# Two-stage attention with a token-mixing MLP: loads moved from two queues with casts in the DMA to one fp32 queue with casts on GpSimd and VectorE

## Chip, cores, metric

One core of a Trainium2 chip. The metric is the device time of one execution in microseconds (us), median of several runs. Each run has a state, fast or slow (slow: over 1.5% above the fastest run of the same kernel on the same chip); comparisons use fast runs. A profile is one execution, and its span is 1.7 to 2.1 us shorter than its run's time.

## The reference

Shapes: batch 8, 8 heads, sequence 576, head dimension 64, 32 latents p per head, model width 512. Everything comes and goes in float32.

```python
def sm_attn(qq, kk, vv):                       # softmax(qq kk^T / 8) vv, per batch and head
    ...
p_packed = sm_attn(p, k, v)                    # 32 latents gather from 576 keys
attn     = sm_attn(q, p_packed, p_packed)      # 576 queries read from 32 latents
x        = attn.transpose(0, 2, 1, 3).reshape(8, 576, 512)
W_tok    = einsum('bsd,btd->bst', x @ w_q, x @ w_k) / 8
out      = maximum(einsum('bst,btd->bsd', W_tok, x), 0) @ w_out
```

## The kernel before

The work of a batch is cut into some forty steps (`kt`: transpose k, `sa`: scores of the latents, `pv`: their weighted sum of v, `qt`/`sc`/`sm`/`at`: the second attention, `wk`/`wq`/`g`/`y`/`mx`: the mixing, `oa`/`ob`: the last product and the store). Each step has a **time** in a table. All steps of all batches are sorted by time plus batch times period, and this sorted list is the program order of every engine. The times order the instructions; they do not delay anything.

```python
    PERIOD = 13.0
    TIMES = {
        "lk": (-17.40,),
        "lq": (-13.25,),
        "vc": (0.00,),
        "kt": (3.88, 5.75, 6.78),
        ...                                                        # cut
    }
    dve_relu = (1, 1, 0, 1)          # 1: VectorE, 0: ScalarE
    dve_out = (0, 0, 1, 1, 0)
    dve_g, dve_y = 1, 1

    def load_k(b):                   # load_q is the same with q
        k_in[b] = inpool.tile([P, NG, R, Dh], bf16, tag="k_sb", name="k_sb")
        nc.gpsimd.dma_start(k_in[b], rows(k, b))      # GpSimd's queue casts fp32 to bf16 in the DMA

    def load_v(b):
        v_in[b] = two.tile([P, NG, R, Dh], fp32, tag="v_in", name="v_in")
        nc.sync.dma_start(v_in[b], rows(v, b))        # SyncE's queue, fp32

    def vc(b, _):
        nc.gpsimd.tensor_copy(v_bufs[b % NV][:, :, :, 0:Dh], v_in[b])
        if b + 2 < B:
            load_v(b + 2)
    ...                                                            # cut
    todo = sorted((t + b * PERIOD, b, name, c)
                  for b in range(B) for name, ts in TIMES.items() for c, t in enumerate(ts))
    with tc.manual_schedule():
        p_transposes(0)              # the p of batches 0 and 1
        n_kt = 0
        for _, b, name, c in todo:
            if b == 0 and name == "pv":
                nc.vector.tensor_copy(p_nat[:, 1:], p_sb[:, 1:])
                for i in range(1, 4):
                    p_transposes(i)  # the p of batches 2 to 7, in front of pv of batch 0
            steps[name](b, c)
            ...                                                    # cut
```

The softmax here doesn't subtract the row's maximum and nothing guards it: scores larger than these inputs give would overflow.

## Time and profile before

| | before |
|---|---|
| time, median (range), 4 runs | 159.64 us (158.26 to 162.23) |
| span of the profile, granted TensorE clock | 159.4 us, 0.959 |
| busy: TensorE, VectorE, ScalarE, GpSimd | 117.9, 103.1, 61.4, 65.3 us |
| DMA, share of 16 engines: casting queue, fp32 queue | 34.3%, 39.7% |
| GpSimd's first weight multiply (L296) of batch 0, of batch 7; end | 29.90, 136.22; 159.4 us |

The times in the last row split the span into a fill, seven periods and a drain. How it, the chain of waits and the windows of this profile are read, the prediction shows.

### The profile page before, as it was taken

Reading aid. Unit: us, or ns where it says so; the run is one execution under the profiler, and the core shown is the slowest. Engines: PE = TensorE matmul, PEld = TensorE weight load, DVE = VectorE, ACT = ScalarE, POOL = GpSimd, SP = SyncE. Lnnn points to the kernel's source line nnn. Section 1 sums busy time; section 2 is a strip of 40 time slices with the busy share of each in tenths; the row PEclk is TensorE's granted clock in tenths of the full one; section 3 lists DMA queues with packets and bytes.
Section 4 is the critical chain, followed back from the end, with each engine's and each line's share of the span. In section 5 each row is a group of like instructions: output and inputs, shape, how many; then the busy total and the mean of one; then the engine's idle time right before and its main releaser. Section 6 shows DMA issues by size and latency. Waiting matters only on the chain.

```text
span 159.4 us, 6466 instructions
## 1 busy us (share of the span) xinstructions
PE 117.9 (74%) x2864; PEld 84.0 (53%) x2864; DVE 103.1 (65%) x239; ACT 61.4 (39%) x130; POOL 65.3 (41%) x72
## 2 busy tenths in 40 slices
PE   1254149828766899489998993799999969978950
PEld 1142137718735686365766862676668657544410
DVE  2538276824594679832997696559859994974630
ACT  3403054701352266024443670257155516433420
POOL 7506700396029703960259229702842350460000
PEclk9999999996999999956999999999999999999996
DMA  4999999999941998399626998995055222536574
GB/s 140 253 349 367 252 312 320 260 213 212 277 175 15 199 248 321 39 236 310 233 70 104 228 333 278 206 219 123 26 128 136 72 66 65 141 86 161 136 208 132
DMA packets 14987, 30.49 MB, mean 191 GB/s; under 512 B 2672, under 2 KB 4464, under 8 KB 14960
## 3 DMA queue, kind: packets, MB, share of 16 engines
q1 hardware_dynamic: 9296, 20.58, 39.7%
q0 software_dynamic: 5664, 9.50, 34.3%
q8 instruction: 22, 0.36, 0.9%
q14 instruction: 5, 0.04, 0.1%
HBM read 30.15 MB, written 9.44 MB: 248 GB/s over the span
## 4 chain that ended last, share of the span: by engine, by line
PE 51%; DVE 17%; issue 12%; DMA 9%; ACT 5%; SPq 2%; DVEq 0%; ACTq 0%
PE out_ps L396 16%; DMA p_sb<-in_p_dram 9%; PE T_ps L200 7%; PE pv_ps L239 7%; PE e_ps L284 4%; DVE relu L354 3%; PE mix_ps L365 3%; PE wq_ps L324 3%; PE aT_ps L305 3%; DVE rs L292 3%; PE e_ps L226 2%; PE wk_ps L313 2%; DVE kT L217 2%; PE g_ps L337 2%; DVE y L108 2%
## 5 line engine op out<-in xcount | busy, mean ns | idle before, releaser
L396 PE MATMUL out_ps<-wout_w,relu 128*128 128x512 bf16 x128 | 36.3, 395 | 0.2 <-issue 0.2
L278 DVE COPY qT<-T_ps 128x768 bf16<-128x768 bf16 x24 | 13.1, 545 | 7.8 <-PE T_ps L200 7.7
L200 PE MATMUL T_ps<-ident,k_sb 128*128 128x128 bf16 x144 | 12.9, 230 | 5.1 <-DVE k_sb L108 3.2
L354 DVE TENSOR_SCALAR relu<-mix_ps 128x512 bf16<-128x512 f32 x24 | 16.0, 667 | 0.4 <-PE mix_ps L365 0.3
L110 ACT ACTIVATE o_sb<-out_ps 128x512 f32<-128x512 f32 x20 | 11.2, 595 | 12.9 <-PE out_ps L396 10.8
L396 PEld LDWEIGHTS <-relu 128*128 128x128 bf16 x128 | 11.5, 102 | 8.6 <-issue 1.6
L217 DVE COPY kT<-T_ps 128x768 bf16<-128x768 bf16 x24 | 12.9, 546 | 4.6 <-PE T_ps L200 4.3
L200 PE MATMUL T_ps<-ident,q_sb 128*128 128x128 bf16 x144 | 13.7, 239 | 0.3 <-DVE qT L278 0.3
L284 PEld LDWEIGHTS <-qT 128*96 128x96 bf16 x192 | 12.1, 124 | 2.9 <-issue 0.2
L200 PEld LDWEIGHTS <-q_sb 128*128 128x128 bf16 x144 | 10.9, 109 | 3.8 <-issue 1.0
L200 PEld LDWEIGHTS <-k_sb 128*128 128x128 bf16 x144 | 9.6, 104 | 6.0 <-DVE k_sb L108 3.7
L108 DVE COPY o_sb<-out_ps 128x512 f32<-128x512 f32 x16 | 10.9, 679 | 2.4 <-ACT o_sb L110 1.8
L356 ACT ACTIVATE rest<-mix_ps 128x256 bf16<-128x256 f32 x8 | 3.1, 384 | 24.0 <-PE mix_ps L372 24.0
L365 PE MATMUL mix_ps<-wqT,y 128*128 128x512 bf16 x32 | 11.8, 385 | 0.4 <-DVE y L108 0.4
L226 PE MATMUL e_ps<-pT,kT 128*32 128x64 bf16 x576 | 9.3, 200 | 2.5 <-issue 1.9
L164 PE MATMUL pT_ps<-ident,p_nat 128*64 128x128 bf16 x32 | 2.3, 313 | 11.2 <-DVE p_nat L429 5.6
L252 POOL TENSOR_TENSOR ppb<-pp,mask 128x256 bf16<-128x256 bf16 x16 | 10.4, 674 | 0.1
L110 ACT ACTIVATE pT<-pT_ps 64x512 bf16<-64x512 bf16 x4 | 4.9, 1255 | 12.0 <-DVE pT L108 12.0
L206 POOL CAST v_bf_85<-v_in 128x2304 bf16<-128x2304 f32 x3 | 6.3, 2113 | 7.3 <-DMA v_in<-in_v_dram 7.3
L307 DVE COPY aT<-aT_ps 128x384 bf16<-128x384 bf16 x24 | 8.3, 346 | 1.3 <-PE aT_ps L305 1.3
L226 PEld LDWEIGHTS <-kT 128*32 128x32 bf16 x576 | 6.2, 100 | 5.5 <-issue 2.2
L313 PE MATMUL wk_ps<-pqk,aT 128*96 128x64 bf16 x96 | 8.7, 217 | 0.2 <-DVE aT L307 0.2
(308 smaller groups left out, 260.2 us busy)
## 6 DMA issues: line engine op xcount, KB each, us to landing
v_in<-in_v_dram SPq DMA_DIRECT2D x8, 1152.0 KB, 10.0
q_sb<-in_q_dram POOLq DMA_DIRECT2D x8, 576.0 KB, 9.2
out_dram<-o_sb SPq DMA_DIRECT2D x24, 192.0 KB, 2.6
k_sb<-in_k_dram POOLq DMA_DIRECT2D x7, 576.0 KB, 7.5
out_dram<-o_sb SPq DMA_DIRECT2D x24, 128.0 KB, 2.6
out_dram<-o_sb SPq DMA_DIRECT2D x24, 64.0 KB, 2.8
k_first<-in_k_dram SPq DMA_DIRECT2D x3, 384.0 KB, 5.8
wout_w<-in_moe_w_out_dram POOLq DMA_DIRECT2D x1, 512.0 KB, 27.6
```

Source lines behind the costliest of these rows:

```text
L108: nc.vector.tensor_copy(o, i)
L110: nc.scalar.activation(o, i, COPY)
L200: nc.tensor.transpose(ps[:, r, G, :], x_sb[:, G, sls[r]:sls[r] + 2, :].rearrange("a r d -> a (r d)"), ident)
L217: nc.vector.tensor_copy(kT, ps)
L226: nc.tensor.matmul(ps[m, r, G], kT[:, r, G, m], pT[:, b, G * NP + pos], start=True, stop=True)
L239: nc.tensor.matmul(ps[m, G, 0:Dh + 1], e1[m, r, G, par, :], v_sb[m, G, s, 0:Dh + 1], start=s == 0 and G == 0, stop=s == R - 1, skip_group_ ...
L278: nc.vector.tensor_copy(qT, ps.rearrange("a r G (pos s) -> a (G pos) r s", s=QP))
L284: nc.tensor.matmul(ps[:, :, h, :], qT[:, h].rearrange("a r s -> a (r s)"), st[b]["ppT"][:, h], start=True, stop=True)
L313: nc.tensor.matmul(ps[:, par, :], st[b]["aT"][:, G, c, par, :], st[b]["pqk"][:, G, Dl:], start=G == 0, stop=G == NG - 1)
L354: nc.vector.tensor_scalar_max(o, i, 0.0)
L365: nc.tensor.matmul(ps, yT[:, j * P:(j + 1) * P], wqT[:, 0:SM], start=True, stop=True)
L396: nc.tensor.matmul(ps, lhsT, wout_w[:, j, :], start=j == 0, stop=j == NJ - 1)
```

## The change

Intent: all loads in fp32 through SyncE's queue, with two staging buffers per tensor, so that GpSimd issues no DMA and k of batch 0 comes first; the casts to bf16 in three pieces per tensor on GpSimd (one piece of q on VectorE); relu, y, g and one output copy per batch to ScalarE; warm-up matmuls in the first batches; new step times that include the casts, among them `pr` for the transposes of the later p groups. The copies behind the transposes of p also get another order of elements (1.2 us each before), and there are fewer output buffers.

```diff
-    PERIOD = 13.0
-    TIMES = { ... }                                   # cut
+    TIMES = (
+        (13.00, {
+            "lk": (-17.28,), "lv": (-11.45,), "lq": (-11.39,),
+            "kc": (-5.13, -4.39, -4.21), "qc": (6.89, 4.50, 3.07), "vc": (0.26, 1.55, -0.98),
+            "kt": (0.00, 0.72, 1.47),
+            ...                                        # cut
+            "pr": (-33.29,),
+        }),
+        (13.04, { "mx": ..., "oa": ..., "ob": ... }),  # cut
+    )
-    dve_relu = (1, 1, 0, 1)
-    dve_out = (0, 0, 1, 1, 0)
-    dve_g, dve_y = 1, 1
+    dve_relu = (0, 0, 0, 0)
+    dve_out = (0, 0, 0, 1, 0)
+    dve_qc = (1, 0, 0)                                 # dve_kc, dve_vc, dve_a2: all 0
+    dve_g, dve_y = 0, 0
+    def load(x, name, b, pieces=1):
+        x_in[name, b] = t = two.tile([P, NG, R, Dh], fp32, tag=name + "_in", name=name + "_in")
+        n = R // pieces
+        for c in range(pieces):
+            nc.sync.dma_start(t[:, :, c * n:(c + 1) * n], rows(x, b)[:, :, c * n:(c + 1) * n])
+    def cast(dve, o, i):
+        (nc.vector if dve else nc.gpsimd).tensor_copy(o, i)
     nc.sync.dma_start(p_sb[:, 0], p_v[:, 0])
+    for x, name in ((k, "k"), (v, "v"), (q, "q")):
+        load(x, name, 0, NC3)
+    ...                                                # the weights; cut
     nc.sync.dma_start(p_sb[:, 1:], p_v[:, 1:])         # the rest of p: last of the first loads
     def p_transposes(g):
+        nc.vector.tensor_copy(p_nat[:, g], p_sb[:, g])
+    def pr(b, _):
+        if b % 2 == 1 and b + 1 < B:
+            p_transposes((b + 1) // 2)
     with tc.manual_schedule():
+        constants()
+        warm_up(4)
         p_transposes(0)
+        warm_up(5)
         for _, b, name, c in todo:
-            if b == 0 and name == "pv": ...            # the p groups 1 to 3; cut
             steps[name](b, c)
+            if (b, name) in early:                     # most steps of batch 0, kt and sa of batch 1
+                warm_up(1)
```

## The prediction

> **What bounds the kernel now.** I read the page first (chain of work that ended last, groups, DMA queues), then the chain in order of time, then the waits, the table of windows and the timelines of GpSimd and TensorE. The page's chain, by engine, says that no one thing is the bound: half of it is TensorE, but 12% is "issue" (TensorE waits for nothing that the profile shows) and 9% is one DMA.
>
> ```profile
> PE 51%; DVE 17%; issue 12%; DMA 9%; ACT 5%; SPq 2%; DVEq 0%; ACTq 0%
> ```
>
> The chain in order of time (start, length, what) shows where these lie.
>
> ```profile
> 3.72 15.13 DMA p_sb<-in_p_dram
> 18.87 0.57 DVE p_nat L429
> ...
> 23.34 2.10 PE pv_ps L239 x125
> ...
> 32.72 3.60 issue
> ...
> 97.14 2.94 issue
> ```
>
> **Fill.** The rest of p is the last of the first loads. It lands at 18.87 us, and three groups of p's transposes stand in TensorE's order before the first pv step, so pv of batch 0 ends at 25.4 us although its scores were ready at 13.6 us. The first attention weight (GpSimd's tensor_tensor of L296) starts at 29.90 us, that of the last batch at 136.22 us, and the span ends at 159.4 us. So the kernel is a fill of 29.9 us, seven periods of 15.2 us (106.3 / 7) and a drain of 23.2 us.
>
> **Period.** What is the least that TensorE needs per batch? From the chain and the groups at full clock: 36 transposes at 0.34 us per six (2.04), e of L226 3 x 0.36 (1.08), pv 1.2, e of L284 3 x 0.34 (1.02), aT 0.5, wk 0.5, wq 0.5, g 0.35, y 0.22, mix 1.1, ppT and pqk 0.33, and 18 out matmuls at 0.215 us (3.87). Together 12.7 us. The windows (columns: length, busy of PE, PEld, DVE, ACT, POOL with counts, granted clock, DMA share, GB/s) show how near the good stretches are, and what spoils the others.
>
> ```profile
> 96.00:98.00 2.00, 1.14 (x79) 0.68 (x77) 1.90 (x6) 0.00 (x0) 2.00 (x3) 1.00 1.05 397
> 98.00:100.00 2.00, 0.00 (x0) 0.00 (x0) 0.40 (x1) 0.00 (x0) 1.98 (x4) 1.00 0.64 102
> 38.00:40.00 2.00, 2.00 (x21) 1.87 (x20) 1.28 (x5) 0.57 (x2) 0.51 (x1) 0.50 1.13 215
> 117.00:131.00 14.00, 12.70 (x353) 9.34 (x352) 11.36 (x28) 6.49 (x15) 4.81 (x6) 1.00 0.38 97
> ```
>
> The last line is a batch with few loads left: 14 us, PE busy 12.7, VectorE 11.4. The first two are a stall: pv stops between two matmuls of one group whose inputs have long been ready, for 2.94 us, right where DMA is full. The third is the other loss: after the 3.60 us stall at 32.72 the granted clock is 0.50, and again at 68 to 74 us.
>
> **Between stages VectorE is a second bound**: from 76.5 to 85 us the chain runs almost wholly through it (kT, rs, relu, o_sb). The costliest of its groups that the change touches:
>
> ```profile
> L354 DVE TENSOR_SCALAR relu<-mix_ps 128x512 bf16<-128x512 f32 x24 | 16.0, 667 | 0.4 <-PE mix_ps L365 0.3
> L206 POOL CAST v_bf_86<-v_in 128x2304 bf16<-128x2304 f32 x3 | 6.3, 2114 | 0.0
> q1 hardware_dynamic: 9296, 20.58, 39.7%
> q0 software_dynamic: 5664, 9.50, 34.3%
> q8 instruction: 22, 0.36, 0.9%
> ```
>
> The queues are at 75% of 16 engines' span together, some 119 us. q8 is the third witness for the stalls: 22 packets of 16 KB are about TensorE's 5,728 instructions at 64 bytes.
>
> **What the Trainium skill says.** (1) "Runtime: NRT & Kernel Launch", section "Instruction fetch mechanics": instructions are streamed in 16 KiB blocks of 256 by DMA and the cost is mostly hidden. The trace agrees on the blocks (0.36 MB in 22 packets) and not on the hiding, if I read the stalls rightly: 0.3 to 0.7 us at pv where DMA is light (114.4, 128.1), 2.9 and 3.6 us where it is full. (2) "SBUF — State Buffer", the box on the SWDGE trap and the shared port pair: a DMA issued from GpSimd needs GpSimd to write descriptors, and a VectorE op in a two-port mode (an fp32 SBUF to SBUF copy) and a GpSimd op shut each other out for a whole instruction. In the trace each GpSimd DMA takes 0.75 us of that engine; nothing in it is long enough to show the lock, since VectorE casts from SBUF only at the start. (3) "DMA: Bandwidth & Descriptors", section "Issuing engines are not separate DMA queues": moving transfers to another queue gives no bandwidth. The trace agrees: full-share windows move 206 to 221 GB/s of bf16 in the casting queue (twice that in fp32 read) and 397 to 410 GB/s in fp32 loads. (4) "TensorE: Matmul & The Clock Gate", Part 1: the clock is halved after an idle window of about 3.4 us. The trace agrees at 38 us, and at 98 us a stall of 2.94 us did not trip it.
>
> **The change part by part.**
> - Fill. The rest of p goes behind k, v, q and the weights, and its transposes behind pv of batch 0. Loads in order: p 0.13 MB lands at 2.9 us as before, then k 1.18 MB at 400 GB/s without the casting queue beside it: about 6 us (the third piece landed at 10.1 before), v 9 us, q 12 us. GpSimd casts k in three pieces (a third of 2.11, 0.70 us each) behind its memsets: about 7 to 9 us. kT and scores by 10, v cast by 11.5, pv until 13 (warm, 1.2 instead of 2.1), q cast 12 to 13.5, sc at 15, exp 0.6, sums and reciprocal 0.9: first weights at about **17.5 us** instead of 29.9, so 12.4 us gained. The warm-up matmuls run in TensorE's idle time.
> - VectorE per batch: less three relu (16.0 us in all), y (5.1), g (2.4), one of two o_sb per batch (5.4), memsets about 2; plus one cast of q at 0.57 (4.6 in all). 103.1 - 30.9 + 4.6 = 76.8, or 9.6 us per batch.
> - ScalarE gets them: 61.4 + 24 x 0.595 + 8 x 0.595 + 4.8 + 2.1 = 87.4, or 10.9 per batch.
> - GpSimd: 65.3 less 13.5 of DMA issues and 16.8 of casts, plus 64 casts of about 0.73 (46.7), 2 for w_out, 3 of memsets: 86.7, or 10.8 per batch. It is near the others but below TensorE.
> - DMA: 28.3 MB of loads at 400 GB/s are 71 us, p and weights 4, stores 9.44 MB at 215 / 0.79 = 272 GB/s are 35: 110 us, or 13.2 per batch in steady state (8.85 + 4.3). Nearly the period itself.
> - Period. TensorE is now the longest engine but DMA: 12.7 plus bubbles, some 13.6 us (14.1 in the good batches before, when VectorE had 11.4). In the first two periods the 5 us of mix and out of earlier batches are missing, but loads (9 us) and GpSimd (10.8) are not: about 12. The lag of a batch's output behind its attention grows by some 7 us in the step times, which fits this.
> - Stalls of instruction fetch: 0.3 to 3.6 before, DMA now busy nearly always, but one data queue instead of two. I choose 1.3 us per period, 9 in all.
> - Drain: at the last weights there is work left of about out of 5, mix and out of 6 and 7 and the tail of attention 7: 3 x 3.87 + 2 x 1.1 + 3.5 = 17.3 us, against about 15.5 before with a drain of 23.2. So 24 to 25.
>
> **Sum**: 17.5 + 2 x 12 + 5 x 13.6 + 9 + 24 = 142.5 of span, and the median lay 0.9 over the profiled span: **143 us**, 17 less than 160.25. Of the 17, 12 come from the fill and some 5 to 6 from the periods (15.2 to 14.4).
>
> **The rivals.**
> - *Instruction fetch takes over.* For it: DMA at 13.2 us per batch is full through the middle, and the worst stalls were in full stretches, one of them (97 us) beside fp32 loads of the SyncE queue, just what will be the rule. Against: stalls lie in pv and the dense scores, and the new times set 12 long matmuls between these. At 3 us per period instead of 1.3, with a clock drop or two: about 155.
> - *GpSimd becomes the bound.* Its casts and weights are in one order; a cast that waits for a late load holds the weights behind it, and VectorE's q cast and GpSimd exclude each other (0.6 us per batch). For it: 10.8 of 13, loads of v and q bunched, stores in the same queue behind them. Against: loads are issued 10 to 14 us ahead. At 15 us per period: 17.5 + 105 + 24 = 146 to 148.
> - *All goes as the step times would have it.* TensorE full, no clock loss, 11.5 in the first two periods and 13 after, fetch hidden: 17.5 + 23 + 65 + 4 + 23 = 133.
> - *Nothing gained*: the early start only shifts the wait to the loads. Against: loads end at 110 us of DMA time whatever the order, well under 143.
>
> **Range and chances.** The second rival and the third mark the sides, the first is the worse tail: 134 to 152. Within 2% or slower would need the fill's 12 us to be lost again in stalls: 0.04 and 0.02. Faster 0.94.
>
> **What would show it.** First weights on GpSimd at 16 to 20 us (fill right); their spacing about 12 in the first two periods and 14 to 15 in the later; PE busy over 12.5 per period; DVE near 77, ACT 87, POOL 87 busy; no software_dynamic queue and DMA share near 1 from 3 to about 85 us; "issue" at pv, near 1.3 us per batch and longer where DMA is full. The prediction is wrong if GpSimd's casts are much over 0.73 us, if GpSimd waits for loads in the middle, or if TensorE waits on kT, qT or v for more than 1 us per batch.

## More of the kernel before

The granted clock is a mean over the clock events that the trace records. The stretch before the first event (26.8 us in before) is counted as full clock, although TensorE's transposes took some 314 ns in it, against 219 later; so the mean is too high.

## The result, and the profile after

| | before | after |
|---|---|---|
| time, median (range), 4 runs each | 159.64 us (158.26 to 162.23) | 171.03 us (169.68 to 173.66) |

The ratio is **1.072** (95% interval 1.057 to 1.087): slower by 7%, where 143 us had been predicted. Ratios here and below are the mean time of one kernel's fast runs over that of the other's fast runs of the same rounds, so not quite the ratio of the medians.

The first profile of the changed kernel fell in the slow state (span 171.9 us, clock 0.887). The kernel was run again unaltered (a_again), and its profile is what is read here. It is the quickest of the changed kernel's eight runs: span 165.2, clock 0.938. So the loss read in it is smaller than in the other runs.

Lines of its page: two DMA queues (packets, MB, share of 16 engines), the chain by engine, and the group of q's casts on VectorE (busy us, mean ns, idle before):

```profile
q1 hardware_dynamic: 16048, 39.59, 71.4%
q8 instruction: 22, 0.36, 0.9%
...
PE 64%; DVE 9%; DMA 9%; issue 8%; POOL 4%; SPq 1%; ACT 1%; POOLq 0%; ACTq 0%
...
L137 DVE CAST q_bf<-q_in 128x768 bf16<-128x768 f32 x8 | 12.7, 1582 | 0.0
```

The casting queue is gone, as predicted. DMA work stayed what it was: 74.0% of 159.4 us before and 71.4% of 165.2 us after are both 118 us, where 110 had been predicted. But the eight casts of q on VectorE took 1582 ns each, not 570.

The chain in order of time (start, length, what):

```profile
8.85 9.14 DMA p_sb<-in_p_dram
18.01 0.30 DVE p_nat L164
18.36 0.64 PE pT_ps L168 x8
18.99 0.75 PE T_ps L213 x6
...
25.23 3.78 issue
...
35.20 1.04 POOL a L318
...
55.56 5.67 DVE p_nat L164
```

Read it against the same lines of before. The rest of p is on the chain again, it lands at 18.0 us as before (18.9), and the transposes of p follow at once. The difference is in what stands *behind* them: here the first transposes of k (T_ps, 18.99 us), which before began at 5.75 us. The first weights come at 35.20 us (before 29.90), those of batch 7 at 141.77 (136.22), the end at 165.2.

| | fill | period, mean of seven | drain | span |
|---|---|---|---|---|
| before | 29.9 | 15.19 | 23.2 | 159.4 |
| predicted | 17.5 | 14.4 | 24 | 142.5 |
| after (a_again) | 35.2 | 15.22 | 23.4 | 165.2 |

**The p transposes.** `pr` of batch 1 has the time -33.29 + 13.00 = -20.29, and `kt` of batch 0 has 0.00. So the p group of batches 2 and 3, needed only by `sa` of batch 2 at 28.5, comes before any work of batch 0 in the sorted list. On TensorE everything waits for the last of the first loads.

**The casts on VectorE.** The timeline of a_again around the 5.67 us step of the chain (start, length, engine; the rows left out are other engines' and one start of a DMA):

```profile
54.69 1.59 POOL L137 CAST v_bf<-v_in 128x768 bf16<-128x768 f32 x2
...
55.47 5.75 DVE L164 CAST p_nat<-p_sb 128x256 bf16<-128x256 f32 x1
...
56.25 1.05 POOL L318 TENSOR_TENSOR a<-e,rr 96x512 bf16<-96x512 f32 x1
...
57.24 0.82 POOL L137 CAST q_bf<-q_in 128x768 bf16<-128x768 f32 x1
58.01 1.73 POOL L384 CAST wout_w<-wout_in 128x512 bf16<-128x512 f32 x3
59.69 0.83 POOL L137 CAST q_bf<-q_in 128x768 bf16<-128x768 f32 x1
60.46 0.61 POOL L384 CAST wout_w<-wout_in 128x512 bf16<-128x512 f32 x1
61.04 1.34 POOL L271 TENSOR_TENSOR ppb<-pp,mask 128x256 bf16<-128x256 bf16 x2
```

The cast of p, 0.29 us when GpSimd is idle (it took 0.30 us at 18.01), lasts from 55.47 to 61.22 us, and all that while GpSimd runs one instruction after another without a gap. TensorE waits 5.30 us for it.

So after the result there were two suspects for the loss (**theory F**, the fill; **theory L**, VectorE's casts shut out by GpSimd) and one for the missing gain (**theory I**, instruction fetch under load, the prediction's first rival).

### The profile page after: what moved, and what is told of

Its sections match the earlier page's. It is cut to its first block, busy times and chain, and to the rows that moved or that the text cites. A ratio compares the mean times of both kernels' runs of the same rounds, so it can differ in the third digit from the quotient of the medians.

```text
span 171.9 us, 6636 instructions
## 1 busy us (share of the span) xinstructions
PE 125.8 (73%) x2878; PEld 88.2 (51%) x2904; DVE 94.8 (55%) x193; ACT 81.0 (47%) x178; POOL 93.3 (54%) x122
## 4 chain that ended last, share of the span: by engine, by line
PE 61%; issue 10%; DMA 9%; DVE 8%; POOL 6%; ACT 1%; SPq 1%; ACTq 0%; POOLq 0%; DVEq 0%
PE out_ps L421 18%; PE T_ps L213 10%; PE pv_ps L258 7%; DMA p_sb<-in_p_dram 5%; PE e_ps L306 4%; DMA v_in<-in_v_dram 4%; PE mix_ps L390 4%; DVE p_nat L164 3%; PE e_ps L245 3%; PE aT_ps L328 3%; PE warm_ps L197 3%; PE wk_ps L336 2%; PE wq_ps L347 2%; DVE q_bf L137 2%; PE g_ps L360 2%
## 5 line engine op out<-in xcount | busy, mean ns | idle before, releaser
L379 ACT ACTIVATE relu<-mix_ps 128x512 bf16<-128x512 f32 x32 | 17.9, 608 | 12.5 <-PE mix_ps L390 12.4
L137 POOL CAST k_bf<-k_in 128x768 bf16<-128x768 f32 x24 | 20.6, 890 | 5.0 <-DMA k_in<-in_k_dram 5.0
L197 PE MATMUL warm_ps<-warm 128*128 128x512 bf16 x33 | 15.8, 522 | 1.2 <-DVE warm L177 1.2
L164 DVE CAST p_nat<-p_sb 128x256 bf16<-128x256 f32 x4 | 7.2, 1808 | 14.1 <-DMA p_sb<-in_p_dram 14.1
L213 PE MATMUL T_ps<-ident,q_bf 128*128 128x128 bf16 x144 | 13.7, 239 | 0.9 <-DVE q_bf L137 0.7
L137 POOL CAST q_bf<-q_in 128x768 bf16<-128x768 f32 x16 | 13.0, 835 | 1.8 <-issue 1.8
L137 DVE CAST q_bf<-q_in 128x768 bf16<-128x768 f32 x8 | 14.0, 1745 | 0.0
L213 PE MATMUL T_ps<-ident,k_bf 128*128 128x128 bf16 x144 | 12.9, 230 | 0.0
L306 PEld LDWEIGHTS <-qT 128*96 128x96 bf16 x192 | 11.9, 127 | 1.0 <-issue 0.4
L213 PEld LDWEIGHTS <-q_bf 128*128 128x128 bf16 x144 | 10.8, 109 | 2.2 <-DVE q_bf L137 0.8
L213 PEld LDWEIGHTS <-k_bf 128*128 128x128 bf16 x144 | 10.1, 105 | 1.6 <-issue 1.0
```

The costliest lines, as they stand in the source:

```text
L137: (nc.vector if dve else nc.gpsimd).tensor_copy(o, i)
L164: nc.vector.tensor_copy(p_nat[:, g], p_sb[:, g])
L197: nc.tensor.matmul(ps, warm[:, 0:P], warm, start=True, stop=True)
L213: nc.tensor.transpose(ps[:, r, G, :], xc[:, G, r].rearrange("a x d -> a (x d)"), ident)
L306: nc.tensor.matmul(ps[:, :, h, :], qT[:, h].rearrange("a r s -> a (r s)"), st[b]["ppT"][:, h], start=True, stop=True)
L379: nc.scalar.activation(o, i, RELU)
```

## The experiments

Twelve kernels, in three calls of four. Kernels of one call share a chip and the runs of the kernel before. All results were correct unless it is said otherwise.

| run | what it is | median us | ratio to before (95%) |
|---|---|---|---|
| (first) | the change | 171.03 | 1.072 (1.057 to 1.087) |
| a_again | the change, again | 173.12, one of 4 fast | none |
| b_pr_late | change, later p transposes behind pv | 164.14 | 1.016 (1.004 to 1.028) |
| c_act_casts | change, VectorE's casts on ScalarE | 164.06 | 1.019 (1.004 to 1.034) |
| d_both | b and c | 157.97 | **0.983** (0.974 to 0.993) |
| e_no_loads | d, no loads after batch 1 (wrong) | 144.42 | 0.905 (0.892 to 0.917) |
| f_pieces3 | d, loads in three DMAs | 160.69 | 1.008 (0.998 to 1.019) |
| g_split_g | d, loads in two DMAs | 157.57 | 0.988 (0.976 to 1.001) |
| h_before_p_late | before, later p transposes behind aT | 162.71 | 1.021 (1.006 to 1.036) |
| i_reduce_casts | b, VectorE's casts by tensor_reduce | 159.55 | 0.999 (0.991 to 1.007) |
| j_no_warm | d, no warm-ups between steps | 160.67 | 1.004 (0.996 to 1.012) |
| k_before_flags | before, the change's engine choices only | 158.51 | 0.990 (0.982 to 0.999) |
| l_no_warm_split | j and g | 163.49, two of 4 fast | none |

### a_again: control

> The changed kernel again, unaltered: control for the others of this call, and a profile that may fall in the fast state (the first one had a span of 171.9 us at a granted clock of 0.887). Expected 170 us, ratio to before 1.065 to 1.075.

Its runs were 166.95, 170.57, 175.67 and 176.90 us, so all but the first count as slow and no ratio was formed. The changed kernel scatters more than before (159.38 to 162.57).

### b_pr_late: theory F

```diff
-            "pr": (-33.29,),
+            "pr": (-5.00,),
```

> One number: the step time of the later p transposes, -33.29 to -5.00, so that the group for batches 2 and 3 comes after pv of batch 0 in every engine's order and no longer before the first k transposes. Theory F (the loss is the fill: the changed kernel's TensorE waits for the rest of p, which is the last of the first loads, before its first k transposes): k transposes start at 7 to 10 us instead of 19.2, first attention weights on GpSimd at 20 to 26 us instead of 36.5, time 157 to 162, ratio 0.99 to 1.02. Theory L (the loss is VectorE's casts from SBUF shut out by GpSimd): within 2 us of the changed kernel, because the lost time is in the middle.

The first k transposes start at 6.56 us, a little before the expected 7 to 10, and the first weights come at 25.84 us. The ratio falls from 1.072 to 1.016, 5.6% of before or some 9 us, about the 9.4 us by which the fill of the profiles shrank (35.20 to 25.84). Theory F holds. The median, 164.1 us, is a little over the expected 157 to 162; the ratio is in its range. In this profile the q casts on VectorE cost more than in a_again (2204 ns in the median, one of 6.91 us, and 8.0% of the chain against 3.7%), so the other loss is still there.

### c_act_casts: theory L

```diff
     def cast(dve, o, i):
-        (nc.vector if dve else nc.gpsimd).tensor_copy(o, i)
+        if dve:
+            nc.scalar.activation(o, i, COPY)
+        else:
+            nc.gpsimd.tensor_copy(o, i)
...                                                    # p_nat of groups 1 to 3 and half of wqk likewise
```

> All casts from SBUF that the changed kernel gives to VectorE once GpSimd is busy (one piece of q per batch, three of the four p casts, half of the w cast) go to ScalarE instead, some 8 x 0.84 us more there. Theory L: 17 us of VectorE waiting in these casts vanish, of which about 6 to 10 lay on the chain (5.6 in p, 3.0 in one q): time 160 to 165, ratio 1.00 to 1.035; the fill stays at 36 us. Theory F: the fill is unchanged, at most 2 us gained.

164.06 us, ratio 1.019, with the fill still at 34.58 us. Some 8 us gained without touching the fill: theory L holds too, with time and ratio inside its ranges.

### d_both: do they add?

> Both edits. If F and L are separate losses they add: time 147 to 153, ratio 0.92 to 0.96. If one hides the other: no better than the better of the two. If the real bound is something else (instruction fetch under a full DMA queue, GpSimd's own stream): above 157.

157.97 us, ratio 0.983: from 1.072, 8.9% of before, against 5.6 and 5.3% for each alone. They add for the most part, but the range expected for that (147 to 153 us) was missed: the time is just above 157, the third case, so something else bounds the kernel as well. Still, nothing more is needed to explain why the change is *slower*: without these two faults it is 1.7% faster than before. But it is 15 us off the prediction. Its profile (slow, span 157.6) has the first weights at 23.76 us.

### i_reduce_casts: is it the port?

Theory L says that the two engines exclude each other. The kernel could also have been slow there for another reason. The Trainium skill ("VectorE: DVE Perf Modes", section "The perf-mode tier table (the rule you actually need)") gives tensor_reduce only the 1x mode, and tensor_copy of fp32 in SBUF the 2x mode. So the same cast, at the same place of the same engine, by a sum over one element:

```diff
         if dve:
-            nc.vector.tensor_copy(o, i)
+            with nc.allow_low_precision(reason="one element each"):
+                nc.vector.tensor_reduce(o.unsqueeze(len(o.shape)), i.unsqueeze(len(i.shape)),
+                                        axis=AX, op=ADD)
...                                                    # p_nat of groups 1 to 3 and half of wqk likewise
```

> b_pr_late with the same casts still on VectorE and at the same places, but done as a sum over one element (tensor_reduce) instead of tensor_copy: an operation that by the skill's table has only the one-port mode, and whose fp32 kin (the row sums of e) never stretched in any trace. Theory L (the two-port mode is shut out by GpSimd): each q cast takes 0.9 to 1.0 us every time instead of 0.56 to 6.9, time 157 to 160, near d_both, although VectorE's own work grows by 3 us. Rival (VectorE's copies are slow there for another reason: load on SBUF from DMA, or VectorE's place in the order): they stretch as before, time 162 to 165.

The tile's views (min/median/max of one instruction in ns), of b_pr_late and then of this kernel:

```profile
L137 DVE CAST q_bf<-q_in x8: 560/2204/6911, 15.2 to 130.4; 128x768 bf16<-128x768 f32 x8
```

```profile
L139 DVE TENSOR_REDUCE q_bf<-q_in x8: 941/942/953, 15.8 to 128.4; 128x768 bf16<-128x768 f32 x8
...
L139 DVE TENSOR_REDUCE p_nat<-p_sb x3: 407/409/409, 20.9 to 86.3; 128x256 bf16<-128x256 f32 x3
L170 DVE CAST p_nat<-p_sb x1: 2836/2836/2836, 2.9 to 2.9; 128x256 bf16<-128x256 f32 x1
```

A form that is slower when alone (942 against 560 ns) is faster where it matters, because it never stretches, and GpSimd's casts of q beside it do not either (818 to 834 ns). The last line is a comparison within the run: the one cast left as a copy took 2.84 us (2.90 to 5.74), beside a memset of 2.65 us on GpSimd (2.94 to 5.59); the same cast took 0.40 us in before. So it is the copy that stretches, and not its place in the order or the loads. That it does so because of its two-port mode is the skill's explanation; the lengths alone (560 against 942 ns) fit it. The ratio, 0.999, is 1.7% of before (some 3 us) better than b_pr_late's, though the two intervals just overlap, and 1.6% short of d_both's. That rest is not settled. In the profiles the fill is longer than d_both's, 27.76 against 23.76 us, with the periods no longer (15.38 against 15.80, d_both's slow); what lengthens it no run tells.

### e_no_loads: theory I

```diff
     def load(x, name, b, pieces=1):
+        if b >= 2:
+            x_in[name, b] = x_in[name, b % 2]
+            return
```

> d_both with the loads of k, q and v of batches 2 to 7 left out (they reuse the buffers of batches 0 and 1: a wrong result on purpose); casts, order and stores as in d_both. Theory I (TensorE's stalls at pv and elsewhere are instruction fetch held up by data on the DMA engines): from 30 us on no issue stall over 1.5 us, their sum under 5 us against 13 in d_both, no clock drop after 30 us, time 140 to 147, ratio 0.88 to 0.92. Rival S (the stalls are the same fetch limit with or without load, or GpSimd's stream is the bound): sum of stalls over 9 us or time above 152.

144.42 us, ratio 0.905: 13 us less than d_both, at the same instructions but the loads. The result is wrong (relative error 1.45). TensorE's waits for issue sum to 7.9 us, of which 2.9 lie in the fill, so 5.0 from 30 us on, at the expected bound of 5; one stall of 1.96 us is over the bound of 1.5. The rest of the expectation was met (the clock falls once more, 1.5 us before the end). Since d_both's profile is slow, g_split_g, which differs from it only in splitting each load and times the same, stands in for the comparison; both profiles below are fast. First the page's busy line of g_split_g:

```profile
PE 121.9 (79%) x2878; PEld 85.8 (56%) x2904; DVE 72.2 (47%) x181; ACT 88.3 (57%) x190; POOL 91.3 (59%) x122
```

and TensorE's waits for "issue" in it (total us, times, longest):

```profile
PE pv_ps L263 <- issue: 9.5, 7, 3.0
PE mix_ps L395 <- issue: 3.3, 5, 2.6
PE T_ps L218 <- issue: 3.0, 1, 3.0
...
PE out_ps L426 <- issue: 1.9, 4, 1.3
```

The same two views of e_no_loads:

```profile
PE 117.9 (83%) x2878; PEld 82.6 (58%) x2904; DVE 71.9 (51%) x181; ACT 88.3 (62%) x190; POOL 91.1 (64%) x122
```

```profile
PE pv_ps L264 <- issue: 4.2, 3, 2.9
PE mix_ps L396 <- issue: 2.6, 5, 2.0
...
PE out_ps L427 <- issue: 1.1, 3, 0.8
```

Stalls: 17.7 against 7.9 us. TensorE busy for the same matmuls: 121.9 against 117.9 us, since the clock fell less without the loads (0.970 against 0.932). These are 9.8 and 4.0 us, and the spans differ by 154.4 - 141.5 = 12.9. Waits for the loads themselves hardly differ: GpSimd's casts wait 7.5 us for them in g_split_g and 6.9 in e_no_loads. The period falls from 15.21 to 13.44 us ((131.00 - 24.55) / 7 and (118.38 - 24.32) / 7), and 13.1 was the prediction's sum without its term for stalls.

That these stalls are instruction fetch, and not a wait that the profile does not see, is shown by where they fall. The windows from 0 to a moment inside a stall count what TensorE has done by then; the second count in brackets is weight loads. Three stalls of before, then three of d_both:

```profile
0.00:34.50 34.50, 15.30 (x479) 12.23 (x480) 18.92 (x43) 12.03 (x17) 14.58 (x21) 1.00 1.04 277
...
0.00:47.20 47.20, 24.28 (x735) 20.07 (x736) 26.32 (x61) 16.29 (x27) 19.63 (x25) 0.96 1.02 264
...
0.00:50.90 50.90, 26.56 (x863) 21.89 (x864) 28.82 (x67) 17.27 (x29) 22.78 (x29) 0.97 0.95 245
```

```profile
0.00:15.50 15.50, 9.70 (x221) 4.91 (x224) 4.21 (x13) 4.19 (x6) 10.61 (x22) 0.93 0.92 276
...
0.00:47.50 47.50, 33.74 (x855) 22.83 (x863) 19.41 (x51) 19.41 (x39) 31.51 (x48) 0.89 0.99 363
...
0.00:79.00 79.00, 60.73 (x1618) 43.62 (x1631) 37.40 (x96) 39.43 (x83) 57.14 (x81) 0.91 0.88 318
```

480, 736 and 864 are 96 plus 3, 5 and 6 times 128; 224, 863 and 1631 are 96 (or 95) plus 1, 6 and 12 times 128. With one matmul to a weight load, 128 of each are 256 instructions, at 64 bytes a block of 16 KB: what one packet of the instruction queue carries. Two kernels with different orders stop at the same counts. Without loads the stalls that remain stand at such counts too (1247, 1631, 2015), so the loads lengthen them but do not make them.

How they lengthen them stands in the trace's list of single DMA packets, which holds the 22 of the instruction queue. In before TensorE passes a block's end at 36.31 us; the next packet starts at 40.04 and ends at 41.01, and TensorE goes on past the next block's end at 42.24. Where the data queues are idle, the same four times are 47.88, 49.02, 50.24 and 51.61. So a block is fetched one ahead, and the loads lengthen the wait before its packet starts: 3.7 against 1.1 us. The packet itself (1.0 and 1.2 us) and the time from its end to TensorE's next instruction (1.2 and 1.4 us) hardly change. At all 22 stalls over 0.6 us of before, d_both and e_no_loads TensorE went on 1.2 to 1.7 us after a packet's end. A kernel that uses up a block of 256 faster than these three times together (5.9 us with loads, 3.7 without) waits.

### f_pieces3 and g_split_g: does the size of a DMA matter?

```diff
-    def load(x, name, b, pieces=1):
+    def load(x, name, b, pieces=3):                    # f_pieces3
```
```diff
-            nc.sync.dma_start(t[:, :, c * n:(c + 1) * n], rows(x, b)[:, :, c * n:(c + 1) * n])
+            for G in range(NG if pieces == 1 else 1):  # g_split_g
+                g = slice(G, G + 1) if pieces == 1 else slice(0, NG)
+                nc.sync.dma_start(t[:, g, c * n:(c + 1) * n], rows(x, b)[:, g, c * n:(c + 1) * n])
```

> d_both with every load of k, q and v in three DMAs of six rows (descriptors of 1536 bytes instead of 4608, a third of the bytes per engine and DMA). Theory P (a fetch waits for the whole share that one DMA has put on its engine, about 74 KB at 25 GB/s or 2.9 us): the longest stalls shrink from 2.9 to about 1.5 us, time 150 to 155. Rival (the fetch waits behind all that is queued, or load efficiency falls with the short descriptors): stalls as in d_both or longer, time 156 to 162.

> d_both with the loads of batches 1 to 7 in two DMAs, one for each half of the heads, at the same descriptor size of 4608 bytes. Theory P: longest stalls shrink to about 2 us, time 153 to 157. Rival: no difference beyond 1 us from d_both (157 to 159).

Theory P fell, and both rivals' ranges were met. The longest stalls of pv stayed at 3.1 and 3.0 us, f_pieces3 is slower than d_both, and g_split_g equals it. In the first 50 us the packets of the instruction queue start 2.7 to 3.8 us after a block's end in d_both, 2.7 to 4.0 in f_pieces3 (both profiles slow) and 2.6 to 3.7 in g_split_g (fast). So a fetch does not wait for one DMA's share; what it waits for behind the loads is open.

### h_before_p_late: did the fill need the new loads?

```diff
-            if b == 0 and name == "pv":
+            if b == 0 and name == "at" and c == 0:     # and behind the step, not in front of it
```

> The kernel before with one edit: the cast and transposes of the later p groups moved from in front of pv of batch 0 to behind the aT transposes of batch 0. If its fill of 29.9 us was held by these too: first attention weights at 20 to 24 us, time 152 to 156, ratio 0.95 to 0.98; so the fill that the change was to shorten could have been had without its loads. If the loads of v and q hold the fill anyway: within 1% of before.

Neither case came. The first weights come at 26.15 us, 3.75 earlier, but the time does not fall (ratio 1.021). The chain in order of time has two new pieces:

```profile
4.57 24.80 DMA q_sb<-in_q_dram
...
35.15 0.79 DVE p_nat L430
35.99 0.66 PE pT_ps L164 x8
...
41.15 1.25 ACT pT L110
```

The first is q of batch 1, issued at 4.57 us by GpSimd's casting queue and landing at 29.4 us; but TensorE waited only 0.8 us for it. The larger piece is the moved p work itself: its cast, transposes and copies now hold the chain from 35.15 to 42.40 us. TensorE was also slower there: most of its transposes take 314 ns up to 46.4 us, where in before most of them take 219 from 26.84 us on. So the edit moved the wait to another place, and the run does not tell whether the shorter fill needs the change's loads. An order for p that is in nobody's way, with the old loads, was not tried.

### k_before_flags: the engine choices alone

```diff
-    dve_relu = (1, 1, 0, 1)
-    dve_out = (0, 0, 1, 1, 0)
-    dve_g, dve_y = 1, 1
+    dve_relu = (0, 0, 0, 0)
+    dve_out = (0, 0, 0, 1, 0)
+    dve_g, dve_y = 0, 0
```

> The kernel before with only the engine choices of the change (three relu, y, g and one o_sb copy per batch from VectorE to ScalarE), its loads, casts and step times kept. If VectorE is the second bound of the good stretches, as the prediction said: VectorE 103 to 73 us busy, periods without heavy loads 13.3 to 13.7 instead of 14.1, time 154 to 158, ratio 0.96 to 0.985. If what is saved is lost in waits for instructions and loads: within 1% of before.

158.51 us, ratio 0.990 (0.982 to 0.999): a gain of 1%, less than the first case expected. VectorE fell to 78.4 us busy. The last two periods, with few loads, did fall, from 14.15 and 13.58 to 13.41 and 12.36 us; but TensorE's stalls for instructions summed to 14.8 us, as before (14.7). Relief of VectorE is real and small.

### j_no_warm and l_no_warm_split

```diff
-            if (b, name) in early:
-                warm_up(1)
```

> d_both without the single warm-up matmuls between the steps of batches 0 and 1 (the nine at the start stay). If they lie on the path (warm matmuls are 3% of d_both's chain) and do not keep the clock, since it falls in the stall at 14 us anyway: 1 to 4 us faster than d_both, 154 to 157. If they keep the clock up: 1 to 4 us slower.

> j_no_warm with the loads in two DMAs as in g_split_g. A candidate for a version that beats both; expected equal to the better of the two within 1 us: 153 to 157, ratio 0.95 to 0.98.

j_no_warm came out as its second case: 160.67 us, some 3 slower than d_both. The expectation of l_no_warm_split failed: it is worse still (its two fast runs, 162.34 and 161.69). The warm-ups are worth 2 to 3 us of d_both. Why is not settled. The clock is lower without them (0.872 against 0.921 in the profiles, d_both's a slow one), but leaving out 31 matmuls also moves every later block boundary, and the stalls at pv grew from 9.9 to 16.4 us. The two are not told apart here.

## Why the prediction was wrong, point by point

- **Fill: wrong, and the step that failed first.** The prediction put the p transposes of the later groups "behind pv of batch 0". The sorted list puts the first of them in front of k of batch 0 (time -20.29 against 0.00), and the second still in front of pv (5.71 against 7.17). Measured: fill 35.2 instead of 17.5 us. With `pr` moved (b_pr_late) GpSimd casts k from 5.69 to 8.05 us, near the predicted 7 to 9, and the time falls by 5.6% of before. The rest of the term was mis-sized: with the fault mended the fill is 24 to 26 us (27.8 in i_reduce_casts). In d_both v was cast from 10.8 us on, q was ready at 14.5 instead of 12, and a fetch stall of 2.33 us lies in pv of batch 0.
- **VectorE's casts: term mis-sized.** The prediction had 0.57 us per q cast and, as a rival's part, 0.6 us of exclusion per batch, and did not look at p and w at all. Measured in a_again: 12.7 us for eight q casts, and 5.75 us for one cast of p. Taken off VectorE, 5.3% of before is gained (c_act_casts); i_reduce_casts shows that it is the copy that stretches. The page on the port had been read and cited; what was missed is that GpSimd's work comes in long runs without a gap (54.7 to 62.4 us in the timeline above) that the loser has to sit out.
- **GpSimd: nearly right, and not the bound.** 93.7 us busy against 87 predicted; a cast took 0.82 to 0.89 us, not 0.73. In g_split_g and e_no_loads the same GpSimd work fits periods of 15.2 and 13.4 us, so the second rival did not happen in the way it was told.
- **DMA: nearly right.** 71.4% of the span in one queue (118 us, as in before) where 110 was the sum.
- **Period without stalls: near.** 13.44 us in e_no_loads, which still has 5.0 / 7 = 0.7 us of stalls in it; the sum was 92 / 7 = 13.1. With loads the shape was wrong too: the first two periods, put at 12 us, took 16.1 and 16.3 in g_split_g (12.5 and 12.7 in e_no_loads).
- **Instruction fetch: the rival that was under-weighted.** 1.3 us per period was chosen. With the two faults mended, the loads cost 15.21 - 13.44 = 1.8 us per period on top of what remains without them (7.9 us in all, fill included): about 10 us in longer stalls and 4 in clock. Of the 11.9 us between g_split_g's span and the predicted 142.5, 7.1 lie in the fill and 5.4 in the periods; the drain gives back 0.6. So the mended kernel stands at 158 and not at 143 first for its longer fill and then for its stalls.
- **Drain: near** (23.4 against 24), but it did not grow as the prediction had it; before it was 23.2.
- **Span to time: slip.** The prediction added 0.9 us to its span. Every run here took 1.7 to 2.1 us more than its own span; the median of before, then 160.25, lay only 0.9 over the profile's span because the profiled execution was one of the longer ones (161.34).

So the change is slower because of its place for the p transposes and because of VectorE's copies beside a busy GpSimd. Both are shown by undoing them. Its aim, a shorter fill, was sound, and d_both (1.7% faster than before, with g_split_g the best correct version here) has it: 23.8 us against 29.9. Whether that needed the new loads is not shown. The step times spent it.

Open: what an instruction fetch waits for behind the loads before its packet starts (splitting the loads did not help), why the warm-ups matter, and whether the old loads with another order for p would do as well.

## What to carry to other kernels

When a schedule is a sorted list, look up what each new step is sorted *in front of*, above all a step whose input is loaded last: its engine will wait there with everything behind it. Keep fp32 copies between two SBUF tiles off VectorE while GpSimd is busy back to back; ScalarE, or even a slower one-port operation, was better here. And where TensorE runs thousands of small instructions, count the blocks of 256: full DMA queues and long stalls come together at their boundaries.

## What the Trainium skill lacked or had wrong

- "SBUF — State Buffer", section "SBUF: two separate sides": it says that the loser of the shared port waits for the other's instruction. The runs show more: VectorE's cast lasted through a row of GpSimd instructions, 5.75 us for 0.29 us of work across eight whole ones, and up to 6.91 us for a q cast. The page does not say that a busy GpSimd can starve VectorE.
- "Runtime: NRT & Kernel Launch", section "Instruction fetch mechanics": it calls the cost of crossing a block mostly hidden. Here TensorE stalled at block boundaries for 14.7 us of 159 in the kernel before, up to 3.6 us at once, and for 7.9 us with the loads of two batches alone; no page links it to the load on the DMA engines, under which a fetch's packet started 3.7 us after the block's end instead of 1.1.
- "TensorE: Matmul & The Clock Gate", Part 1: it warns that recorded clock events are unreliable. These runs do not show it: of the 271 transposes of a_again that fall under a clock record, 270 have the length that goes with it (some 311 ns at half clock, 219 at full). What misleads is the stretch before the first record, 21.74 us there: the views print 1.00 for it, while most transposes took 311 to 314 ns. That is the view's doing, not the record's.
